# One block's weight conversions in a new order: a list for each step, more of them by hand at the start, and a place of their own for the narrowed chunks

## The chip, the cores and the metric

The kernel runs on one core of a Trainium2 chip. The metric is device time in microseconds; the median of three runs before the change is 604.85 us (604.66 to 604.88).

## The reference

Chunked attention, then a feed-forward layer with a rational activation, then a soft mixture of experts. With x the attention's output as 3072 tokens of 512:

```
h = x @ w_in                                   # 512 -> 2048
P = a0 + a1*h + a2*h^2 + a3*h^3
Q = 1 + |b0|*|h| + |b1|*h^2
g = P / (Q + 1e-6)
x2 = g @ w_out                                 # 2048 -> 512
logits = x2 @ phi                              # 512 -> 32 slots
d = softmax over tokens; c = softmax over slots
slot_out = experts(d.T @ x2);  out = c @ slot_out
```

w_in and w_out come in as float64. [...]

## The kernel before, in words

The 3072 tokens are 6 blocks of 512, and a block has 8 steps, one for each 256 of the 2048 columns of h. A step is numbered kk over all blocks; the first block is steps 0 to 7.

In a step, TensorE (PE) computes the **next** step's h (`h0`, `h1`: twelve 128x128x512 matmuls each, x and w_in each split into a high and a low part, L321). ScalarE (ACT) and VectorE (DVE) make the rational function of **this** step's h: `a1` is ACT L540, L541, L543 and DVE L542; `d1` is DVE L553, L554; `a2` is ACT L559, L560; `t` is DVE L570, L571 for the step before, after a product on GpSimd (POOL, L517). `p0`, `p1` transpose the finished g (L347, copied by ACT L348) and multiply it into the logits (L340). `at` runs one slice of the next block's attention; a block has two pairs of heads' tiles, 18 slices a pair: scores on PE (L164), softmax on DVE and ACT (L182, L185, L186, L190 to L192), transposes (L201, copied by ACT L205), values (L214), DVE L224, transposes (L233), and the copies into the next block's x, ACT L237 and DVE L238. At `h0` of a block's last step all slices that are left are run.

Only the first block also converts the weights, chunk by chunk (i = 0 to 7):

- `i`, `o`: load a chunk of w_in (L291) or w_out (L296) into one of four buffers of the pool `g`.
- `s` (split_w): f64_narrow (ACT L278, DVE L279, ACT L280, DVE L282) makes float32, then ACT L304 and DVE L305 the high and low part that h needs. h of step i reads chunk i.
- `n` (narrow_w_out): the same f64_narrow on a chunk of w_out, into one of three scratch tiles that are taken in turn; POOL L312 stores it to DRAM for the end of the kernel.
- `w` (wp_chunk), `z` (wp_sum): eight PE transposes of the narrowed chunk (L416), two ACT copies into a tile of pool S (L417), eight PE products with phi (L424), and one small ACT copy (L425). The logits need chunk i of it.

What sets the order: up to `start.close()` PE, ACT, DVE and POOL follow the program's order as written (table `pre`, which advances several generators in turn). After it the tile layer sorts each engine's instructions by a priority and by its own planning, so the rows printed below as the order are what counts. Each engine works through its own list strictly in order; an instruction that waits holds all behind it on that engine. Before, one list (`ord0`) with relative chunk numbers served all eight steps of the first block.

## Time and profile before

| | |
|---|---|
| median of 3 runs | 604.85 us |
| profiled execution, its own time | 606.56 us |
| its span, first to last instruction | 604.8 us |
| PE busy | 546.7 us, 90% |
| DVE busy | 454.2 us, 75% |
| ACT busy | 417.9 us, 69% |
| POOL busy | 125.3 us, 21% |
| a1 of step 0 / 1 / 5 / 8 starts at | 47.87 / 59.29 / 114.27 / 150.04 us |

The shares are averages over stages with different limits. The first block ends near 150 us; the five others take some 73 us each. PE's busy time counts a matmul from its start to a modelled end, so in the first block, where matmuls wait for little things between them, it reads fuller than it is.

### The profile page before, as it was taken

Reading aid. Unit: us, or ns where it says so; the run is one execution under the profiler, and the core shown is the slowest. Engines: PE = TensorE matmul, PEld = TensorE weight load, DVE = VectorE, ACT = ScalarE, POOL = GpSimd, SP = SyncE. Lnnn points to the kernel's source line nnn. Section 1 sums busy time; section 2 is a strip of 40 time slices with the busy share of each in tenths; the row PEclk is TensorE's granted clock in tenths of the full one; section 3 lists DMA queues with packets and bytes.
Section 4 is the critical chain, followed back from the end, with each engine's and each line's share of the span. In section 5 each row is a group of like instructions: output and inputs, shape, how many; then the busy total and the mean of one; then the engine's idle time right before and its main releaser. Section 6 shows DMA issues by size and latency. Waiting matters only on the chain.

```text
span 604.8 us, 13444 instructions
## 1 busy us (share of the span) xinstructions
PE 546.7 (90%) x5832; PEld 381.3 (63%) x5832; DVE 454.2 (75%) x559; ACT 417.9 (69%) x542; POOL 125.3 (21%) x65
## 2 busy tenths in 40 slices
PE   2679899979999999999999999999999997889981
PEld 2567676657767777677766777767777675435220
DVE  4667999987987988978889798897987969610031
ACT  2568999986877868778687777877778778410041
POOL 0000132122213133131331313223133315100000
PEclk9969899998999999999999999999999999788996
DMA  7975887230220222112122022220275235799938
GB/s 296 413 271 189 336 293 264 83 127 0 107 71 29 78 70 106 70 37 80 63 106 70 21 87 71 105 71 22 87 279 191 88 140 181 290 369 407 409 133 333
DMA packets 21755, 97.41 MB, mean 161 GB/s; under 512 B 3136, under 2 KB 3136, under 8 KB 16704
## 3 DMA queue, kind: packets, MB, share of 16 engines
q1 hardware_dynamic: 19728, 92.28, 41.2%
q0 software_dynamic: 1152, 4.19, 1.7%
q8 instruction: 46, 0.75, 0.5%
q10 hardware_dynamic: 816, 0.07, 0.1%
q14 instruction: 13, 0.11, 0.0%
HBM read 86.05 MB, written 10.49 MB: 160 GB/s over the span
## 4 chain that ended last, share of the span: by engine, by line
PE 54%; ACT 18%; DVE 13%; issue 5%; DMA 5%; POOL 2%; SPq 0%; DVEq 0%; ACTq 0%; POOLq 0%
PE h L321 28%; PE m L398 4%; ACT S L540 4%; ACT S L541 3%; ACT g L348 3%; PE lg L340 3%; PE m L347 3%; PE m L214 3%; DVE T L553 2%; PE h L640 2%; PE m L233 2%; POOL S L517 2%; PE m L201 2%; DMA xt<-in_kw_dram 2%; DMA T<-in_moe_w_dram 2%
## 5 line engine op out<-in xcount | busy, mean ns | idle before, releaser
L321 PE MATMUL h<-xt,win 128*128 128x512 f32 x1152 | 296.5, 405 | 7.7 <-ACT win L304 5.9
L321 PEld LDWEIGHTS h<-xt,win 128*128 128x128 f32 x1152 | 212.1, 191 | 56.2 <-ACT win L304 8.3
L517 POOL TENSOR_TENSOR S<-S,S 128x1024 f32<-128x1024 f32 (+1 forms) x49 | 118.9, 2428 | 317.1 <-DVE S L542 304.1
L540 ACT ACTIVATE S<-h,ctab 128x1024 f32<-128x1024 f32 (+1 forms) x49 | 53.9, 1100 | 58.7 <-PE h L321 56.6
L542 DVE SCALAR_TENSOR_TENSOR S<-S,S 128x1024 f32<-128x1024 f32 (+1 forms) x49 | 58.8, 1200 | 42.9 <-ACT S L541 42.7
L553 DVE TENSOR_TENSOR T<-T,h 128x1024 f32<-128x1024 f32 (+1 forms) x49 | 58.4, 1192 | 6.7 <-ACT T L543 6.7
L570 DVE SCALAR_TENSOR_TENSOR T<-T,ctab,S 128x1024 f32<-128x1024 f32 (+1 forms) x49 | 63.3, 1294 | 0.0
L347 PEld LDWEIGHTS m<-ident,T 128*128 128x128 f32 x384 | 44.0, 144 | 28.9 <-issue 13.4
L571 DVE SCALAR_TENSOR_TENSOR T<-S,T 128x1024 f32<-128x1024 f32 (+1 forms) x49 | 59.8, 1220 | 3.2 <-POOL S L517 0.5
L554 DVE SCALAR_TENSOR_TENSOR T<-T,ctab,h 128x1024 f32<-128x1024 f32 (+1 forms) x49 | 61.3, 1250 | 0.7
L543 ACT ACTIVATE T<-h,ctab 128x1024 f32<-128x1024 f32 (+1 forms) x49 | 59.2, 1208 | 0.0
L348 ACT ACTIVATE g<-m 128x512 f32<-128x512 f32 x96 | 53.8, 607 | 3.8 <-PE m L347 3.7
L560 ACT ACTIVATE S<-S,ctab 128x1024 f32<-128x1024 f32 (+1 forms) x49 | 55.9, 1140 | 0.8
L559 ACT ACTIVATE S<-S 128x1024 f32<-128x1024 f32 (+1 forms) x49 | 51.6, 1054 | 6.8 <-DVE S L542 5.1
L347 PE MATMUL m<-ident,T 128*128 128x128 f32 x384 | 54.3, 282 | 1.4 <-DVE a L185 1.2
L541 ACT ACTIVATE S<-h,ctab 128x1024 f32<-128x1024 f32 (+1 forms) x49 | 54.2, 1105 | 0.6 <-DVE T L570 0.6
L340 PE MATMUL lg<-T,wp 128*32 128x512 f32 x192 | 40.7, 618 | 3.9 <-DVE T L571 3.8
L398 PE MATMUL m<-g,ptok 128*32 128x512 f32 x192 | 23.5, 634 | 0.4 <-ACT ptok L390 0.4
L186 ACT ACTIVATE a<-a 128x512 f32<-128x512 f32 x22 | 13.8, 640 | 14.1 <-DVE a L185 14.1
L693 DVE TENSOR_SCALAR win<-h,csum 128x512 f32<-128x512 f32 x12 | 8.0, 744 | 20.4 <-PE m L687 20.4
L214 PE MATMUL m<-v,a 64*32 64x64 f32 x1408 | 20.8, 233 | 2.7 <-issue 2.5
L238 DVE TENSOR_TENSOR xt<-m,xt 128x512 fp32r<-128x512 f32 x24 | 16.3, 687 | 7.9 <-ACT xt L237 7.8
(152 smaller groups left out, 601.3 us busy)
## 6 DMA issues: line engine op xcount, KB each, us to landing
win<-in_moe_w_dram SPq DMA_DIRECT2D x32, 512.0 KB, 5.0
k<-in_kw_dram SPq DMA_DIRECT2D x11, 1024.0 KB, 7.4
v<-in_vw_dram SPq DMA_DIRECT2D x11, 1024.0 KB, 4.9
g<-in_moe_w_in_dram SPq DMA_DIRECT2D x8, 1024.0 KB, 6.5
g<-in_moe_w_out_dram SPq DMA_DIRECT2D x8, 1024.0 KB, 8.9
out_dram<-win SPq DMA_DIRECT2D x12, 512.0 KB, 6.1
q<-in_qw_dram SPq DMA_DIRECT2D x11, 512.0 KB, 3.7
T<-in_moe_w_dram SPq DMA_DIRECT2D x10, 512.0 KB, 10.3
```

The lines of the kernel that those rows point to most:

```text
L321: PE.matmul(tile_[:, f2, :], lhsT=ww[:, c, f2 * P:f2 * P + P], rhs=xx[:, c, :], start=(n == 0), stop=(n == 3 * NC - 1))
L340: PE.matmul(st["lg"][32 * j:32 * j + 32, :], lhsT=wp[:, 4 * qd + j, :], rhs=gt_tile[k - 1 + j // 2][:, j % 2, :], start=(qd == 0), stop=(q ...
L347: PE.transpose(pb[:, m, f2 * P:f2 * P + P], t_[:, f2, tt * P:tt * P + P], ident)
L348: ACT.activation(gts[b, qd][:, 2 * part:2 * part + 2, 2 * P * o:2 * P * o + 2 * P], pb, AF.Copy)
L517: POOL.tensor_tensor(out[:, o], q[:, o], w[:, o], ALU.mult)
L540: ACT.activation(s[:, o], hh[:, o], AF.Abs, scale=b0)
L541: ACT.activation(y[:, o], hh[:, o], AF.Square, scale=rb1)
L543: ACT.activation(t[:, o], hh[:, o], AF.Identity, bias=a2, scale=a3)
L553: DVE.tensor_tensor(t[:, o], t[:, o], hh[:, o], ALU.mult)
L554: behind[kk] = DVE.scalar_tensor_tensor(t[:, o], t[:, o], a1, hh[:, o], ALU.add, ALU.mult).ins
L570: DVE.scalar_tensor_tensor(t[:, o], t[:, o], a0, w[:, o], ALU.add, ALU.mult)
L571: DVE.scalar_tensor_tensor(t[:, o], e[:, o], 2.0, t[:, o], ALU.subtract, ALU.mult, reverse0=True)
```

## The change

- Each narrowed w_out chunk gets a tile of its own from the pool `win` (16 buffers) where three scratch tiles went round before. split_w takes its two `win` tiles only after narrowing.
- f64_narrow yields once more, between DVE L279 and ACT L280, so that a generator can be advanced in three pieces before its end.
- `pre` now holds, in hand order: the first two pairs' attention, splits of chunks 0 to 2, narrowing of w_out chunks 0 and 1, wp of chunk 0, and both halves of step 0's h. The loads of the next block's q and v move from `loads` into `pre`, behind those of w_in and w_out chunk 2.
- `ord0` is a list for each step, with absolute chunk numbers. The last conversion stands in step 4; before, the last ones stood in steps 6 and 7. Of 36 attention slices 15 stand in steps 0 to 4 and 21 in steps 5 to 7; before, six stood in each step.

```
-    'loads': "q0 q1 v0 i0 v1 o0 i1 o1 q2 v2".split(),
-    'pre': "A A B B A A A A A A A A A A B B B B s B B A A B B s A A A A s B B n t B B B B B B n t t".split(),
-    'pre2': "i2 w0 z0 o2 n1 i3".split(),
-    'ord0': "at a1 w1 s2 h0 d1 at t o3 z1 i4 n2 at a2 h1 p0 at p1 at at".split(),
+    'loads': "q0 q1 v0 i0 v1 o0 i1 o1".split(),
+    'pre': ("A A B B A A A A A A A A A A B B B B s B B s A A B B s A A A A n n B B B B s i2 t B B B B t n n o2 t q2 v2 "
+            "N N h0 t i3 w0 N N o3 h1 u u u u i4 z0").split(),
+    'ord0': [x.split() for x in (
+        "at a1 n2 o4 h0 d1 t s3 i5 a2 w1 h1 z1 p0 p1",
+        "at a1 n3 o5 h0 d1 t s4 i6 w2 a2 n4 o6 h1 z2 p0 at p1",
+        "at a1 n5 o7 w3 h0 d1 t at s5 i7 z3 w4 a2 h1 z4 p0 at p1",
+        "at a1 n6 w5 h0 d1 t at s6 z5 a2 h1 p0 at p1 at",
+        "at a1 n7 w6 h0 d1 at t s7 z6 at w7 a2 h1 z7 p0 at p1 at",
+        "at at a1 h0 d1 at t at a2 h1 p0 at p1 at at",
+        "at at a1 h0 d1 at t at a2 h1 p0 at p1 at at at",
+        "at a1 h0 d1 at t at a2 h1 p0 at p1 at at")],
...
         DVE.tensor_scalar(f, f, -F64_HI, F64_HI, ALU.max, ALU.min)
+        yield
         ACT.activation(f, f, AF.Prelu, scale=2.0 ** -112, alpha=-(2.0 ** 32))
...
-    scratch = [p_win("win", [P, 1024]) for _ in range(3)]
...
-        wh, wl = win[i] = [p_win("win", [P, NC, 2 * P], F32R) for _ in range(2)]
         src = stage_in.pop(i)
         yield from f64_narrow(src[:, :, :, 1], src)
+        wh, wl = win[i] = [p_win("win", [P, NC, 2 * P], F32R) for _ in range(2)]
...
-        f = scratch[i % 3].rearrange("p (j d) -> p j d", j=2)
+        f = p_win("win", [P, 1024]).rearrange("p (j d) -> p j d", j=2)
...
-            "s": split_w(0), "n": narrow_w_out(0), "t": split_w(1)}
-    for what in KN["pre"]:
-        next(gens[what], None)
...
+            "s": split_w(0), "t": split_w(1), "u": split_w(2), "n": narrow_w_out(0), "N": narrow_w_out(1)}
...
+    for what in KN["pre"]:
+        if what in gens:
+            next(gens[what], None)
+        elif what[0] == "h":
+            if what == "h0":
+                hs[0] = ps_h("h", [P, 2, BLK])
+            h_part(0, hs[0], int(what[1]))
+        elif what[0] in "qv":
+            load(what)
+        else:
+            convert(what)
...
-            convert(what[0] + str(min(i + int(what[1]), NSTEP)))
+            convert(what)
```

The lines of the changed kernel stand 8 to 10 further down: L278 becomes L286, L280 L289, L304 L312, L305 L313, L417 L425, L424 L432, L425 L433, L540 L550, L542 L552.

**PE, h of step 0.** h_592 before and h_559 after are the same tile; win_415 and win_416 (win_521 and win_522) are chunk 0's two parts, L416 (L424) are wp's transposes and L424 (L432) its products. Before:

```order
L321 MATMUL h_592<-xt_150,win_416 128x512 x2
L416 MATMUL m_561<-ident_103,win_145 128x128 x4
L416 MATMUL m_567<-ident_103,win_145 128x128 x4
L321 MATMUL h_592<-xt_150,win_416 128x512
L424 MATMUL m_573<-u_107,S_560 128x32 x4
L321 MATMUL h_592<-xt_150,win_416 128x512
L321 MATMUL h_592<-xt_150,win_415 128x512 x4
L321 MATMUL h_592<-xt_151,win_415 128x512
L424 MATMUL m_573<-u_107,S_560 128x32 x4
L321 MATMUL h_592<-xt_151,win_415 128x512 x3
L321 MATMUL h_592<-xt_150,win_416 128x512 x4
```

After:

```order
L329 MATMUL h_559<-xt_147,win_522 128x512 x4
L424 MATMUL m_579<-ident_103,win_448 128x128 x4
L424 MATMUL m_585<-ident_103,win_448 128x128 x4
L329 MATMUL h_559<-xt_147,win_521 128x512 x4
L329 MATMUL h_559<-xt_148,win_521 128x512 x4
L329 MATMUL h_559<-xt_147,win_522 128x512 x4
L432 MATMUL m_617<-u_107,S_578 128x32 x4
```

The products with phi, which stood inside the second half of h, now stand behind it.

**ACT, from a1 of step 2 on.** S and T are the rational function's tiles, g_... loaded chunks, a_4 attention. Before (h_809 is step 2's h):

```order
L540 ACTIVATE S_948<-h_809,ctab_105 128x1024
L541 ACTIVATE S_950<-h_809,ctab_105 128x1024
L280 ACTIVATE g_728<-g_728 128x1024
L543 ACTIVATE T_949<-h_809,ctab_105 128x1024
L278 ACTIVATE g_740<-g_740 128x1024
L280 ACTIVATE g_740<-g_740 128x1024
L417 ACTIVATE S_955<-m_956 128x512
L417 ACTIVATE S_955<-m_962 128x512
L278 ACTIVATE g_831<-g_831 128x1024
L425 ACTIVATE wp_106<-m_997 128x64
```

After (h_789):

```order
L286 ACTIVATE g_702<-g_702 128x1024
L289 ACTIVATE g_702<-g_702 128x1024
L433 ACTIVATE wp_106<-m_932 128x64
L425 ACTIVATE S_942<-m_943 128x512
L425 ACTIVATE S_942<-m_949 128x512
L569 ACTIVATE S_955<-S_873 128x1024
L433 ACTIVATE wp_106<-m_970 128x64
L570 ACTIVATE S_955<-S_955,ctab_105 128x1024
L312 ACTIVATE win_926<-g_702 128x1024
L194 ACTIVATE a_4_867<-a_4_867 128x8x64
L550 ACTIVATE S_986<-h_901,ctab_105 128x1024
```

Two wp chunks and chunk 5's split now stand between the a1 of steps 2 and 3, and the second wp copy has one full instruction between it and the copies whose product it reads.

**DVE, up to the last copies into the next block's x (xt).** T_1590 after belongs to step 7, a_9 to the last attention pair. Before:

```order
L282 SCALAR_TENSOR_TENSOR win_146<-g_1288 128x1024
L238 TENSOR_TENSOR xt_618<-m_1478,xt_617 128x16x32
L238 TENSOR_TENSOR xt_618<-m_1516,xt_617 128x16x32
L542 SCALAR_TENSOR_TENSOR S_1523<-S_1525,S_1523 128x1024
L553 TENSOR_TENSOR T_1524<-T_1524,h_1444 128x1024
L305 TENSOR_TENSOR win_1437<-g_1167,win_1436 128x1024
```

After:

```order
L552 SCALAR_TENSOR_TENSOR S_1589<-S_1591,S_1589 128x1024
L199 TENSOR_SCALAR sm_1474<-sm_1474 128x8
L232 TENSOR_TENSOR a_9_1587<-m_1519,sm_1468 128x8x64
L200 RECIPROCAL sm_1474<-sm_1474 128x8
L563 TENSOR_TENSOR T_1590<-T_1590,h_1452 128x1024
L232 TENSOR_TENSOR a_9_1587<-m_1520,sm_1474 128x8x64
L564 SCALAR_TENSOR_TENSOR T_1590<-T_1590,ctab_105,h_1452 128x1024
L580 SCALAR_TENSOR_TENSOR T_1446<-T_1446,ctab_105,S_1478 128x1024
L246 TENSOR_TENSOR xt_629<-m_1597,xt_628 128x16x32
L246 TENSOR_TENSOR xt_629<-m_1604,xt_628 128x16x32
```

Before, the copies into xt stood ahead of step 6's own work and of the last conversion; now the conversion is long done and the copies stand behind most of step 7.

## Rows read from the trace of the kernel before

**Rows 1.** Windows: us, busy us (count) of PE, PEld, DVE, ACT, POOL; clock; DMA.

```profile
59.30:114.30 55.00, 50.29 (x510) 37.64 (x509) 51.64 (x62) 52.05 (x67) 12.79 (x8) 0.97 0.70 249
151.40:500.00 348.60, 344.68 (x3761) 252.01 (x3761) 298.32 (x345) 271.19 (x346) 89.76 (x38) 1.00 0.25 89
```

**Rows 2.** Chain that ended last, 30 to 155 us: start, us, what.

```profile
30.28 1.23 DVE win L305
31.50 1.21 DVE g L279 x2
...
33.96 1.98 PE m L233 x8
...
36.62 4.63 PE h L321 x10
...
43.07 0.81 PE m L424 x8
...
46.15 1.69 PE h L321 x7
...
119.76 2.89 DVE g L279
...
136.35 2.50 DVE win L305
138.89 10.58 PE h L321 x40
...
151.48 0.92 PE m L164 x61
```

**Rows 3.** Timeline of ACT, step 0: start, us, instruction, idle before.

```profile
47.87 1.11 ACT L540 ACTIVATE S<-h,ctab 128x1024 f32<-128x1024 f32 x1 [1.45 <-PE h L321]
...
49.88 1.21 ACT L543 ACTIVATE T<-h,ctab 128x1024 f32<-128x1024 f32 x1
50.97 0.60 ACT L417 ACTIVATE S<-m 128x512 f32<-128x512 f32 x1
51.44 1.19 ACT L278 ACTIVATE g<-g 128x1024 uint32<-128x1024 uint32 x1
...
55.10 1.06 ACT L559 ACTIVATE S<-S 128x1024 f32<-128x1024 f32 x1
56.05 1.12 ACT L304 ACTIVATE win<-g 128x1024 fp32r<-128x1024 f32 x1
57.05 0.23 ACT L425 ACTIVATE wp<-m 128x64 f32<-128x64 f32 x1
...
58.24 1.14 ACT L560 ACTIVATE S<-S,ctab 128x1024 f32<-128x1024 f32 x1
59.29 1.09 ACT L540 ACTIVATE S<-h,ctab 128x1024 f32<-128x1024 f32 x1
```

**Rows 4.** Timeline of ACT, a1 of step 5.

```profile
114.27 1.14 ACT L540 ACTIVATE S<-h,ctab 128x1024 f32<-128x1024 f32 x1
```

**Rows 5.** Timeline of DVE: half-width and full-width instructions one behind another.

```profile
87.36 1.28 DVE L238 TENSOR_TENSOR xt<-m,xt 128x512 fp32r<-128x512 f32 x2
...
146.22 1.23 DVE L542 SCALAR_TENSOR_TENSOR S<-S,S 128x1024 f32<-128x1024 f32 x1 [3.67 <-ACT S L541]
147.36 1.22 DVE L553 TENSOR_TENSOR T<-T,h 128x1024 f32<-128x1024 f32 x1
148.62 1.28 DVE L554 SCALAR_TENSOR_TENSOR T<-T,ctab,h 128x1024 f32<-128x1024 f32 x1
149.81 1.28 DVE L570 SCALAR_TENSOR_TENSOR T<-T,ctab,S 128x1024 f32<-128x1024 f32 x1
```

**Rows 6.** Timeline of PE: h at full clock, transposes behind a pause, matmuls behind a pause.

```profile
33.96 1.97 PE L233 MATMUL m<-ident,T 128*128 128x128 f32 x8 [3.41 <-DVE T L224]
...
69.75 3.27 PE L321 MATMUL h<-xt,win 128*128 128x512 f32 x7 [2.33 <-ACT win L304]
...
152.33 3.01 PE L321 MATMUL h<-xt,win 128*128 128x512 f32 x12
```

**Rows 7.** Windows again: the granted clock (eighth number group) in two low stretches.

```profile
35.00:40.00 5.00, 4.31 (x13) 3.23 (x12) 3.65 (x4) 3.55 (x5) 0.73 (x1) 0.50 0.39 131
70.00:75.00 5.00, 5.00 (x137) 3.73 (x137) 5.00 (x8) 5.00 (x7) 0.00 (x0) 0.67 0.64 234
```

**Rows 8.** Waits, ACT, 59.3 to 114.3 us: who waited for whom, us, times, longest.

```profile
ACT wp L425 <- PE m L424: 2.7, 3, 1.0
```

More of the change, by code (lines that the diff above doesn't have):

```diff
@@ L455, in tile_chunk_attention__rational__soft_moe @@
     gens = {"A": attention(0, after=NPAIR), "B": attention(1, lambda shape: p_T("T", shape), after=NPAIR),
-            "s": split_w(0), "n": narrow_w_out(0), "t": split_w(1)}
-    for what in KN["pre"]:
-        next(gens[what], None)
-    for gen in gens.values():
-        for _ in gen:
-            pass
-    start.close()
-    for what in KN["pre2"]:
-        load(what) if what[0] in "qv" else convert(what)
+            "s": split_w(0), "t": split_w(1), "u": split_w(2), "n": narrow_w_out(0), "N": narrow_w_out(1)}
     total = NBLK * NSTEP
     hs, gt_tile = {}, {}
-    hs[0] = ps_h("h", [P, 2, BLK])
-    h_part(0, hs[0], 0)
-    h_part(0, hs[0], 1)
+    for what in KN["pre"]:
[9 more added lines that the diff above has]
+            convert(what)
+    for gen in gens.values():
+        assert next(gen, None) is None
+    start.close()
     state = {"att": None}
@@ L593, in tile_chunk_attention__rational__soft_moe @@
             state["att"] = attention_block(b + 1)
-        for what in KN["ord0" if b == 0 else "ord" if b < NBLK - 1 else "ordz" if kk == total - 1 else "ordl"]:
+        for what in KN["ord0"][i] if b == 0 else KN["ord" if b < NBLK - 1 else "ordz" if kk == total - 1 else "ordl"]:
             run_step(kk, what)
```

## Prediction

> **What bounds the kernel now.** I read the windows first. From 151.4 us on PE is busy 344.68 of 348.60 us at full clock [rows 1]: five of the six blocks run at PE's pace, the change touches none of their instructions, and whatever the first block gains or loses is passed on whole. So the question is when PE gets to the point where both kernels do the same again: h of step 8 is done, and the scores of the next attention pair (L164) begin. Before, that is 151.48 [rows 2].
>
> The chain of waits, read in order of time, says what set it. Up to 36.62 the first two pairs' attention ends, with DVE's row of small work on the way to the transposes at 33.96; then h of step 0 with wp's products inside it [rows 2]. From there it lies almost wholly on ACT: in the window 59.3 to 114.3 ACT is busy 52.05 of 55.00 us [rows 1], and the largest of its waits is for wp's products, 2.7 us in three [rows 8]. Near the end it leaves ACT twice for DVE: L279 of 2.89 us, and L305 of 2.50, behind which PE starts h of step 7 at 138.89 and runs on through h of step 8 [rows 2]. So: startup, then ACT, then the last conversion.
>
> ACT's work in the first block is the same before and after, instruction for instruction. The change can win only by starting it earlier, by filling ACT's waits, or by shortening what follows the last conversion. I go through the stages with prices taken from neighbours' starts, since ACT overlaps them by about 0.1 us [rows 3]: a1 and a2 of a step together 5.1 us (L540 and L541 2.01, L543 1.09, L559 0.95, L560 1.05); a narrowing activation 1.19 long, so 1.07; L304 1.0; L417 0.47; L425 0.1 (0.23 long); the half-width attention and g copies 0.5, priced as L417.
>
> **Startup.** On DVE one L305 and one L279 no longer stand ahead of the last attention copies: 1.23 + 0.6 = 1.8 us earlier [rows 2], so h of step 0 starts at 34.8 for 36.62. The high part of chunk 0 is written later than before (ACT now narrows w_out chunk 0 first), but by my count of ACT's list at 32.6, before the x it is multiplied with. The first twelve matmuls fall in the low clock: ten took 4.63 [rows 2], so 5.6; eight transposes (1.97 at the low clock [rows 6], half at the full one; I take 1.2) and the other twelve, at the full-clock rate of 3.01 [rows 6], end h at 44.6. Wp's products, of which the chain has two pieces of 0.81 [rows 2], are no longer inside. So a1 of step 0 stands at 44.6 for 47.87 [rows 3]: 3.3 us won.
>
> **Step 0 to 1.** ACT's list holds a1 and a2 (5.1), five narrowing activations (5.35), one L304, one L425 and two L417: 12.5, and I count 0.6 of wait for a product on PE: a1 of step 1 at 57.7 for 59.29. Two narrowing activations more have been put in there, so this is still ahead.
>
> **Steps 1 to 4, the dense stretch.** Between a1 of step 1 and a1 of step 5 ACT's list now holds four steps' a1 and a2 (20.4), 18 narrowing activations (19.3), five L304 (5.0), twelve L417 (5.6), seven L425 (0.7) and eleven half-width copies (5.5): 56.5 us; all conversions are in it. ACT's waits come on top. Before they were 55.00 - 52.05 = 2.95 [rows 1]. Following the list I find more: the L425 of wp chunks 1, 4 and 6 have one full instruction between them and the copies that feed their product, less than the products take (0.6 + 1.35 + 0.6 by the list), and two copies of g wait for transposes that stand behind pieces of h (1.1 + 1.4): 5.4 with small ones. I take the middle, 4.2, since ACT's first pieces may overlap better than my list shows. So a1 of step 5 stands at 57.7 + 56.5 + 4.2 = 118.4, for 114.27 [rows 4]. It is later because more was done before it.
>
> **Steps 5 to 8.** Here the change moves the bound. No conversion is left, but 21 of 36 attention slices are, and the last copies into x (L238, two) stand on DVE behind most of step 7; h of step 8 needs them. DVE's list from step 5's L542 (2.1 us behind a1) to the last of them has 14 full-width instructions at 1.2 (three intervals of 3.59 from 146.22 to 149.81) and eleven half-width ones at 0.64 [rows 5], and 0.5 of tiny ones, an estimate: 24.3 us, nearly gapless, since ACT and PE hand it the operands about when it is free. That ends at 118.4 + 2.1 + 24.3 = 144.8. Of h of step 8 twenty matmuls follow, 5.0 at full clock [rows 6], and four transposes, 0.5: 150.3, which is 1.2 before 151.48 [rows 2].
>
> **Clock.** PE then has a pause of about 3.4 us (values of the last pair done, waiting for two L224 on DVE), transposes, and h. The nearest row is 33.96: a pause of 3.41 us, eight transposes [rows 6], and then ten matmuls in 4.63 with the clock at 0.50, that is 1.2 GHz; later in the same h seven took 1.69 [rows 2, 7]. The same ten slow ones here lose 10 x (0.46 - 0.25) = 2.1 us. The other bound is 138.89, 40 matmuls in 10.58 where the full rate gives 10.0 [rows 2, 6]: 0.6. I take 2.1, because the pause ahead is like the first row's. The Trainium skill (TensorE: Matmul & The Clock Gate, section "HAM oscillation — how this bites in real kernels") counts half of the time at the lower clock as lost. By it the 4.63 would cost an estimated 2.3, and the sum would be 0.2 higher; the matmul rows agree with it.
>
> **What costs nothing.** No load ends a wait of ACT before, and chunks are now asked for at their buffer's last reader, far ahead of use; the cover is the two or three us that each list has before the chunk's narrowing, and a late one would cost its lateness. Its own tile for each w_out chunk takes a wait for a store off DVE and puts a similar one at the last split, where DVE has 3 us of slack. The long L279 and L305 (2.89 and 2.50 [rows 2], where a neighbour of L305 takes 1.23 [rows 2]) ran while POOL multiplied; the new list has one such neighbour pair, in step 1, under ACT's work. Their going is in the sum, which uses undisturbed prices.
>
> **Sum.** -1.2 + 2.1 = +0.9 us. On the profiled span of 604.8 that is 605.7; the execution itself took 606.56, 1.76 more than its span and 1.71 more than the median, so I put the shift on the median of 604.85: **605.8 us**. Its own range, with ACT's waits between 2.95 and 5.4, the clock term between 0.6 and 2.1, and 1 us of error in the list either side, is 602.0 to 608.0. That is a forecast of nothing that can be told: about 0.2% (1.2 us) is what a measurement of this kernel separates from no change. The 3.3 us won at the start and what the last conversion no longer holds up go into the longer stretch with DVE at the end.
>
> **Rivals.**
> *PE runs free: faster.* In the dense stretch h is ready long before ACT needs it, so products may be done whenever ACT comes to copy them; then ACT's waits lie between 0 and 2.95, and if PE keeps its clock the last part costs no extra. The end is 57.7 + 56.5 + 1.5 + 31.9 (2.1 + 24.3 + 5.0 + 0.5) = 147.6, 3.9 earlier: 601.0, between 599.5 and 602.5. For it: ACT waited little in a similar list before [rows 8], and the two long DVE instructions on the old chain go. Against: the distances of one instruction in the new list.
>
> *The clock falls in the dense stretch: slower.* PE now waits for ACT's L417 in steps 2, 3 and 4 with all of h done. At 69.75 a pause of 2.33 us was followed by seven matmuls in 3.27 [rows 6], where the full rate gives 1.75, at a mean clock of 0.67 [rows 7]: 1.5 a pause. I count four pauses of 2.0 to 3.2 us. If each delays the product that ACT waits for, the sum grows by 6.0 to 611.8. It decides from the point where the pause outlasts the instructions that ACT has between copy and L425. Against it: two of the four have two or more instructions of cover.
>
> *It doesn't do what it says.* The scheduler could have put the conversions back; the printed order shows that it didn't, so no chance goes there.
>
> **Chances.** Forecast 0.48 (0.05 of it faster by over 0.2%, 0.21 the same, 0.22 slower), free PE 0.36, falling clock 0.16. That gives faster 0.41, the same 0.21, slower 0.38. Both signs are open; the likeliest case's own range stands above. The range for 8 in 10 goes from 599.5, the free PE's lower end, to 609.5, which leaves out the upper half of the falling clock.
>
> **What would show it.** Right: a1 of step 0 at 44 to 45.5, of step 1 near 57.7, of step 5 at 117 to 120, last L305 before 123; a PE pause of 3 to 4 us ahead of the last attention transposes, a clock under 0.8 in the window around h of step 8, and L164 behind it at 152 to 154. Free PE: a1 of step 5 before 116.5 and no low clock. Falling clock: windows under 0.8 between 65 and 115 and L425 waits above 6 us. The forecast is wrong at its root if ACT isn't the bound between steps 1 and 5, or if something past 155 us moves.

## The result, and the profile after

The changed kernel takes 610.43 us (median of 5 runs, 607.63 to 611.06). The kernel before took 604.88 beside it (5 runs, 604.66 to 606.15). The ratio is 1.008, with an interval of 1.0059 to 1.0101: slower by 0.8%, where 605.8 us was forecast and the range ended at 609.5. The two profiled executions are 4.1 us apart (610.64 with a span of 608.9, against 606.56 with 604.8), the medians 5.6.

In the changed kernel the lines are shifted: a1's first instruction L540 is L550, wp's copy L417 is L425, its products L424 are L432 and their copy L425 is L433, h is L329, the copies into x L246, the g copies L356, the scores L172. Here are a1 of steps 0, 1, 5 and 8 on ACT (start, us, instruction, idle before and its releaser), to be read against [rows 3, 4]:

```profile
43.15 1.12 ACT L550 ACTIVATE S<-h,ctab 128x1024 f32<-128x1024 f32 x1 [0.18 <-PE h L329]
56.09 1.11 ACT L550 ACTIVATE S<-h,ctab 128x1024 f32<-128x1024 f32 x1
...
121.79 1.12 ACT L550 ACTIVATE S<-h,ctab 128x1024 f32<-128x1024 f32 x1
...
155.59 1.11 ACT L550 ACTIVATE S<-h,ctab 128x1024 f32<-128x1024 f32 x1 [6.60 <-PE h L329]
```

The start is 4.7 us earlier than before (43.15 for 47.87) and 3.2 us at step 1. By step 5 it is 7.5 us late (121.79 for 114.27). Of these 7.5 the forecast had 4.1 (118.4 for 114.27), because more conversions stand ahead of step 5 now; the other 3.4 are the miss. Steps 5 to 8, which hold no conversion any more, win back 3.1. The windows after (columns as in [rows 1]; the third from the end is the granted clock):

```profile
56.09:121.79 65.70, 59.13 (x441) 47.97 (x441) 52.70 (x54) 57.60 (x75) 13.36 (x9) 0.90 0.54 196
155.86:500.00 344.14, 339.22 (x3734) 247.37 (x3734) 293.71 (x341) 266.96 (x340) 89.07 (x37) 1.00 0.25 87
```

```profile
65.00:70.00 5.00, 3.50 (x17) 3.51 (x18) 5.00 (x5) 5.00 (x7) 0.59 (x1) 0.61 0.83 282
70.00:75.00 5.00, 5.00 (x21) 4.20 (x21) 5.00 (x7) 5.00 (x7) 0.53 (x1) 0.70 0.98 400
...
95.00:100.00 5.00, 5.00 (x20) 4.47 (x20) 4.88 (x6) 4.21 (x7) 0.31 (x1) 0.50 0.26 105
...
145.00:150.00 5.00, 4.47 (x16) 3.93 (x17) 5.00 (x6) 2.07 (x4) 0.52 (x1) 0.50 0.00 2
150.00:155.00 5.00, 5.00 (x20) 4.02 (x19) 0.18 (x1) 0.00 (x0) 0.00 (x0) 0.85 0.00 0
```

ACT is busy 57.60 of the 65.70 us between those two a1 and idle 8.10, where before it was idle 2.95 of 55.00 [rows 1]. Behind 155.86 the kernel is the old one again: PE busy 339.22 of 344.14 at full clock. Now the clock stands at 0.50, the 1.2 GHz level, from 95 to 100 and again from 145 to 150, and it is low from 65 to 75. What ACT waited for between 57 and 122 us (us in total, times, longest):

```profile
ACT wp L433 <- PE m L432: 3.9, 4, 1.3
ACT g L356 <- PE m L355: 3.4, 3, 1.4
ACT S L425 <- PE m L424: 0.6, 1, 0.6
```

Before, L425's waits for the same products were 2.7 [rows 8]. The chain of waits, which lay almost wholly on ACT before, now runs through PE from 66.50 to 84.16 and from 92.68 to 103.75. Some of its rows:

```profile
66.50 3.62 PE m L432 x16
...
92.68 1.23 PE m L432 x8
94.39 1.55 PE m L432 x8
95.94 1.33 PE m L355 x6
97.27 0.85 PE h L329 x2
```

The pauses ahead of two of these rows, by the timeline of PE:

```profile
66.50 3.62 PE L432 MATMUL m<-u,S 128*128 128x32 f32 x16 [4.07 <-ACT S L425]
...
92.68 1.23 PE L432 MATMUL m<-u,S 128*128 128x32 f32 x8 [1.98 <-ACT S L425]
```

Sixteen wp products take 3.62 us at 66.50, behind a pause of 4.07, and from 92.68 on, behind a pause of 1.98, wp's products, transposes and pieces of h come one by one while ACT waits. These two are the only pauses of PE over half a microsecond between a1 of step 1 and a1 of step 5. The end of the block, on PE (start, us, instruction):

```profile
145.53 1.97 PE L241 MATMUL m<-ident,a 128*128 128x128 f32 x8 [3.76 <-DVE a L232]
147.29 1.06 PE L355 MATMUL m<-ident,T 128*128 128x128 f32 x4
148.19 7.30 PE L329 MATMUL h<-xt,win 128*128 128x512 f32 x24
155.33 0.60 PE L355 MATMUL m<-ident,T 128*128 128x128 f32 x4
155.86 0.86 PE L172 MATMUL m<-k,q 64*32 64x64 f32 x64
```

The last two copies into x run on DVE from 147.77 to 149.05, h of step 8 waits for them, and L172 follows at 155.86, 4.4 us behind the 151.48 of before [rows 2].

### The profile page after: what moved, and what is told of

Same layout as the page of the kernel before. It is cut to its first block, busy times and chain, and to the rows that moved or that the text cites. A ratio compares the mean times of both kernels' runs of the same rounds, so it can differ in the third digit from the quotient of the medians.

```text
span 608.9 us, 13436 instructions
## 1 busy us (share of the span) xinstructions
PE 546.1 (90%) x5832; PEld 384.7 (63%) x5832; DVE 450.5 (74%) x559; ACT 418.8 (69%) x542; POOL 123.9 (20%) x65
## 4 chain that ended last, share of the span: by engine, by line
PE 55%; ACT 16%; DVE 13%; DMA 5%; issue 5%; POOL 2%; SPq 0%; DVEq 0%; ACTq 0%; POOLq 0%
PE h L329 28%; PE m L355 4%; PE m L406 4%; ACT S L550 4%; ACT S L551 3%; ACT g L356 3%; PE lg L348 3%; PE m L432 3%; PE m L222 3%; DVE T L563 2%; PE h L650 2%; PE m L209 2%; POOL S L527 2%; DVE T L564 2%; PE m L241 2%
## 5 line engine op out<-in xcount | busy, mean ns | idle before, releaser
L329 PE MATMUL h<-xt,win 128*128 128x512 f32 x1152 | 295.2, 405 | 2.9 <-ACT xt L245 1.7
L329 PEld LDWEIGHTS h<-xt,win 128*128 128x128 f32 x1152 | 213.3, 192 | 50.2 <-DVE T L564 2.3
L527 POOL TENSOR_TENSOR S<-S,S 128x1024 f32<-128x1024 f32 (+1 forms) x49 | 117.5, 2398 | 338.9 <-DVE S L552 324.0
L552 DVE SCALAR_TENSOR_TENSOR S<-S,S 128x1024 f32<-128x1024 f32 (+1 forms) x49 | 58.8, 1200 | 53.1 <-ACT S L551 52.9
L550 ACT ACTIVATE S<-h,ctab 128x1024 f32<-128x1024 f32 (+1 forms) x49 | 53.9, 1101 | 61.4 <-PE h L329 58.3
L355 PEld LDWEIGHTS m<-ident,T 128*128 128x128 f32 x384 | 45.5, 147 | 28.4 <-issue 14.4
L356 ACT ACTIVATE g<-m 128x512 f32<-128x512 f32 x96 | 54.0, 603 | 8.0 <-PE m L355 7.7
L355 PE MATMUL m<-ident,T 128*128 128x128 f32 x384 | 55.8, 286 | 3.4 <-DVE a L193 2.3
L348 PE MATMUL lg<-T,wp 128*32 128x512 f32 x192 | 38.4, 608 | 4.6 <-DVE T L581 4.5
L432 PEld LDWEIGHTS m<-u,S 128*128 128x128 f32 x128 | 18.3, 219 | 10.1 <-ACT S L425 9.7
L432 PE MATMUL m<-u,S 128*128 128x32 f32 x128 | 18.7, 297 | 6.6 <-ACT S L425 6.5
(152 smaller groups left out, 598.7 us busy)
```

The lines of the kernel that those rows point to most:

```text
L329: PE.matmul(tile_[:, f2, :], lhsT=ww[:, c, f2 * P:f2 * P + P], rhs=xx[:, c, :], start=(n == 0), stop=(n == 3 * NC - 1))
L355: PE.transpose(pb[:, m, f2 * P:f2 * P + P], t_[:, f2, tt * P:tt * P + P], ident)
L356: ACT.activation(gts[b, qd][:, 2 * part:2 * part + 2, 2 * P * o:2 * P * o + 2 * P], pb, AF.Copy)
L527: POOL.tensor_tensor(out[:, o], q[:, o], w[:, o], ALU.mult)
L550: ACT.activation(s[:, o], hh[:, o], AF.Abs, scale=b0)
L552: DVE.scalar_tensor_tensor(s[:, o], y[:, o], QC, s[:, o], ALU.add, ALU.add)
```

## The experiments

Two causes stood against each other first. Theory A: the late attention loses, since 21 of 36 slices lie in steps 5 to 8 and PE has to wait for the last of them. Theory B: the dense conversions lose, since ACT waits among them. A stand-in, below, is a matmul added to the program whose result is overwritten unread: work beyond the reference. All ratios are to the kernel before, on the same chip and beside it. Its median was 604.88 beside the changed kernel (5 runs each) and 605.6 to 606.0 beside the others (16 to 25 runs); the first line is the last of these batches. "Clock missing" is the sum over the twenty-one 5-us windows from 55 to 160 of 5 us x (1 - granted clock). It is that of one execution, the profiled one, which need not be the median: e1's took 612.63.

| kernel | us, median (range) | ratio to before | clock missing |
|---|---|---|---|
| before | 605.82 (604.3 to 607.1) | 1 | 3.4 |
| changed | 610.43 (607.6 to 611.1) | 1.0080 [1.0059, 1.0101] | 10.2 |
| e6_late | 612.75 (611.7 to 614.1) | 1.0114 [1.0082, 1.0146] | 8.6 |
| e1_spread | 605.16 (604.3 to 612.6) | 1.0000 [0.9971, 1.0029] | 18.8 |
| e2_paced | 604.44 (601.9 to 606.2) | 0.9970 [0.9950, 0.9990] | 8.5 |
| e12_two | 612.14 (610.9 to 617.3) | 1.0122 [1.0088, 1.0155] | 8.5 |
| e4_hold | 605.95 (605.4 to 607.8) | 1.0003 [0.9988, 1.0018] | 6.8 |
| e5_order | 609.27 (608.4 to 610.5) | 1.0063 [1.0046, 1.0079] | 10.2 |
| e17_order4 | 608.90 (607.2 to 610.9) | 1.0057 [1.0037, 1.0078] | 10.2 |
| e7_dense_hold | 606.82 (605.6 to 607.9) | 1.0019 [1.0008, 1.0031] | 5.1 |
| e9_zlater | 606.80 (604.6 to 609.5) | 1.0020 [1.0004, 1.0036] | 8.7 |
| e15_sum | 602.38 (601.5 to 603.9) | 0.9948 [0.9931, 0.9964] | 1.7 |
| e10_spread_hold | 600.37 (599.1 to 602.3) | 0.9917 [0.9899, 0.9936] | 1.7 |
| e8_paced_hold | 600.03 (598.7 to 600.8) | 0.9902 [0.9884, 0.9919] | 3.4 |
| e16_half | 605.89 (604.5 to 607.3) | 1.0000 [0.9989, 1.0012] | 6.8 |
| e11_inpause | 607.57 (605.3 to 609.8) | 1.0030 [1.0013, 1.0047] | 13.7 |
| e14_paced2 | 600.88 (599.3 to 603.4) | 0.9921 [0.9898, 0.9944] | 3.4 |
| e13_before_hold | 607.10 (604.5 to 609.2) | 1.0023 [1.0004, 1.0043] | 5.2 |

### Late attention, or dense conversions

**e6_late** is the kernel before with the change's distribution of attention slices alone (1, 2, 3, 4, 5, 7, 8, 6 in steps 0 to 7, for six in each):

```diff
-    'ord0': "at a1 w1 s2 h0 d1 at t o3 z1 i4 n2 at a2 h1 p0 at p1 at at".split(),
+    'ord0': one list for each step, the same but for the number of "at"
```

> The kernel before, with the attention slices of the first block counted as in the change (1, 2, 3, 4, 5, 7, 8, 6 by step) and nothing else changed. Theory A: slower by 3 to 6 us, 608 to 611, with a pause of PE ahead of h of step 8. Theory B: within 1.5 us of before, 603.5 to 606.5, since the conversions of the last steps hold PE up anyway.

**e1_spread** is the changed kernel with six slices in each step and everything else of the change:

```diff
-        "at a1 n2 o4 h0 d1 t s3 i5 a2 w1 h1 z1 p0 p1",
+        "at a1 n2 o4 h0 d1 at t s3 i5 at a2 w1 h1 z1 p0 at p1 at at",
...
-        "at at a1 h0 d1 at t at a2 h1 p0 at p1 at at at",
+        "at a1 h0 d1 at t at a2 h1 p0 at p1 at at",
```

> The changed kernel, with six attention slices in each step of the first block as before (18 or so fall into steps 0 to 2), the conversions where the change put them. Theory A, late attention: the change loses because 21 of 36 slices stand in steps 5 to 7, so that DVE's list ends 25 us behind a1 of step 5's L542 and PE stands still ahead of h of step 8. Then the pause ahead of step 8's h goes, h of step 8 follows h of step 7 at once, and the time falls by 4 to 6 us, to 604 to 607. Theory B, dense conversions: the loss is ACT's waits in steps 1 to 4. Then a1 of step 5 only comes later, by the 3 us of attention that ACT has to do earlier, what is won at the end is spent ahead of it, and the time stays at 608 to 611.

**e2_paced** spreads the conversions too: own places and the new start of the change, but one w_out chunk and at most one split a step, six slices in each:

```diff
+        "at a1 n2 o4 h0 d1 at t s3 i5 at a2 w1 h1 z1 p0 at p1 at at",
+        "at a1 n3 o5 h0 d1 at t s4 i6 at a2 w2 h1 z2 p0 at p1 at at",
+        "at a1 n4 o6 h0 d1 at t s5 i7 at a2 w3 h1 z3 p0 at p1 at at",
+        "at a1 n5 o7 h0 d1 at t s6 at a2 w4 h1 z4 p0 at p1 at at",
+        "at a1 n6 w5 h0 d1 at t at a2 z5 w6 h1 z6 p0 at p1 at at",
+        "at a1 n7 w7 h0 d1 at t s7 at a2 h1 z7 p0 at p1 at at",
```

> The changed kernel with its start and its own places, but from step 0 on one chunk of w_out and one split a step (w_out chunks 2 to 7 in steps 0 to 5, splits 3 to 6 in steps 0 to 3 and split 7 in step 5, one wp chunk a step, two in step 4), and six attention slices a step. Theory A: as with the attention spread alone, 604 to 607. Theory B: ACT's waits in steps 1 to 4 fall from some 8 us to about 3, and the early start is kept: 599 to 603, faster than the kernel before.

Late attention alone costs 1.1%, some 7 us, more than A expected, and taking it out of the change gives back 0.8%. That is A's result twice, and e6 has the pause ahead of step 8 that A named, although there the clock stays at 1.00 behind it. On PE in e6:

```profile
150.56 1.09 PE L241 MATMUL m<-ident,a 128*128 128x128 f32 x8 [3.01 <-DVE a L232]
```

B's number for e1 (608 to 611) is excluded, and e2 fell short of B's 599 to 603. But e1's profiled execution was the longest of its ten, 612.63 with the clock at 0.50 to 0.58 from 65 to 75, 85 to 100 and 120 to 130. Over the whole execution its mean granted clock was 0.939; the nine others had 0.955 to 0.972 and took 604.3 to 606.7. So there was a third suspect, TensorE's clock.

### The pause ahead of step 8

**e4_hold** is the changed kernel with 14 stand-ins, put between the last products of the attention values and the transposes:

```diff
+                    if nxt == NSTEP:
+                        for n in range(14):
+                            PE.matmul(hs[nxt][:, n % 2, :], lhsT=win[7][0][:, n % NC, 0:P], rhs=xt[0][0][:, n % NC, :],
+                                      start=True, stop=True)
+                        while state["att"] is not None:
+                            slice_()
```

> The changed kernel with 14 stand-in matmuls 128x128x512 in front of the last attention slices of the first block, written to the bank that h of step 8 overwrites; they fall into PE's pause ahead of step 8's h. If the low clock behind that pause costs what the rows say, h of step 8 falls from 7.30 us to about 5.8, the window around it shows a clock near 1.00, and the time falls by 1 to 2 us. If the clock there costs nothing (theory: h waits for x anyway), the time stays within 0.5 us.

It gave back 4.7 us by the ratios (0.0077 of 605.8), more than I expected of the clock. But the scheduler also changed its order: 20 score products of block 1 (L172) now stand inside h of step 8. Two more kernels were to separate the two, the same edit with 1 and with 4 stand-ins.

> e4_hold took back about 4.5 of the 5.6 us by which the changed kernel is behind. Two things were in it: the work of TensorE ahead of step 8 that held the clock, and a new order on TensorE, in which the first score products of block 1 (L172) and one of step 9's products stand inside step 8's products instead of behind them. This kernel keeps the order as far as it goes and has one stand-in product instead of the fourteen. If the clock was the gain: 609 to 610.5, with the granted clock at 0.5 to 0.85 around step 8's products and their 24 taking 7 us or more. If the order was: 605.5 to 606.5 all the same. If each had its part: 607 to 608.5.

> e4_hold with 4 stand-in products instead of 14: the order on TensorE around step 8 is that of e4_hold (20 score products of block 1 inside step 8's products), and some 2.7 us of the pause ahead of step 8 stay. If e4_hold gained by the order: 605.5 to 606.5. If by the clock: 608.5 to 610, with a granted clock of 0.5 to 0.85 around step 8's products. In between: both.

With one stand-in the order fell back to the changed kernel's, so e5 says nothing on the order; it is a second copy of the changed kernel (1.0063), and against it e4's gain is 3.6 us. With four the order behind the stand-ins is that of e4_hold, ACT's and DVE's too, and most of the gain is gone (1.0057): the clock's number, not the order's. Windows 145 to 150 and h of step 8 in e17 and then in e4:

```profile
145.00:150.00 5.00, 5.00 (x21) 4.27 (x19) 4.29 (x5) 1.80 (x3) 0.00 (x0) 0.50 0.00 0
```

```profile
144.63 1.97 PE L241 MATMUL m<-ident,a 128*128 128x128 f32 x8 [3.10 <-DVE a L232]
...
147.29 2.07 PE L329 MATMUL h<-xt,win 128*128 128x512 f32 x4
```

```profile
145.00:150.00 5.00, 4.09 (x42) 3.14 (x42) 5.00 (x6) 2.52 (x5) 0.59 (x1) 1.00 0.02 7
```

```profile
145.60 1.09 PE L241 MATMUL m<-ident,a 128*128 128x128 f32 x8 [0.82 <-DVE a L232]
...
147.43 1.19 PE L329 MATMUL h<-xt,win 128*128 128x512 f32 x4 [0.30 <-ACT xt L245]
```

The pause of 3.10 us with 4 stand-ins leaves the clock at 0.50; filled to 0.82, it stays at 1.00, and eight transposes take 1.09 for 1.97. From a1 of step 5 to a1 of step 10 is 49.90 us in the changed kernel, 49.61 in e17 and 47.51 in e4. So 2.1 us of these 2.4 are the clock, which is the value that the prediction's clock term had, and 0.3 the order. The rest of the gain by the ratios lies outside this stage, and the traces do not say where. The Trainium skill (TensorE: Matmul & The Clock Gate, section "HAM oscillation — how this bites in real kernels") counts half of the time at the lower clock as lost; the windows of e17 from 140 to 155 stand at 0.85, 0.50 and 0.97, which by that rule would be an estimated 3.4 us. The trace gives 2.1; part of the time at the low clock is the pause itself (PE is busy 1.90 of the 5.00 us from 140 to 145), where nothing is lost.

### ACT's waits in the dense stretch

**e7_dense_hold** puts stand-ins ahead of the products of wp chunks 2 and 5; **e9_zlater** moves the products of chunks 2 to 7 one or two places further behind the copies that feed them:

```diff
# e7_dense_hold
+        for n in range({2: 14, 5: 8}.get(i, 0)):
+            PE.matmul(pb_, lhsT=win[0][0][:, n % NC, 0:P], rhs=xt[0][0][:, n % NC, :], start=True, stop=True)
# e9_zlater
-        "at a1 n3 o5 h0 d1 t s4 i6 w2 a2 n4 o6 h1 z2 p0 at p1",
-        "at a1 n5 o7 w3 h0 d1 t at s5 i7 z3 w4 a2 h1 z4 p0 at p1",
-        "at a1 n6 w5 h0 d1 t at s6 z5 a2 h1 p0 at p1 at",
-        "at a1 n7 w6 h0 d1 at t s7 z6 at w7 a2 h1 z7 p0 at p1 at",
+        "at a1 n3 o5 h0 d1 t s4 i6 w2 a2 n4 o6 h1 p0 at p1",
+        "at a1 z2 n5 o7 w3 h0 d1 t at s5 i7 w4 a2 z3 h1 p0 at p1",
+        "at a1 z4 n6 w5 h0 d1 t at s6 a2 h1 p0 z5 at p1 at",
+        "at a1 n7 w6 h0 d1 at t s7 w7 z6 at a2 h1 p0 z7 at p1 at",
```

> The changed kernel with 14 stand-in products ahead of the second chunk's wp products and 8 ahead of the fifth's (into the bank that those products then fill), where TensorE paused 4.1 and 2.0 us and the granted clock was 0.61 to 0.70 and 0.50 behind it. Theory C, the ACT waits of the dense stretch that the prediction missed come from the low clock behind the pauses: the wait for the g copies around 101 to 104 and for the product at 96 go, a1 of step 5 starts at 119 to 120 instead of 121.8, and the time is 607.5 to 609. Theory D, they come from where copy, product and copy stand on the two queues: a1 of step 5 at 121.5 or later and 610 to 611.

> The changed kernel with the products of wp chunks 2 to 7 one or two list places later, so that ScalarE has other work between its copy of a chunk (L425) and the copy of the product (L433). Theory D (the waits come from the places): the four waits of L433 in steps 1 to 5, 3.9 us in all, fall below 1.5, a1 of step 5 starts at 119 to 120 and the end of the block comes as much earlier: 607 to 609. Theory C (low clock): the waits move to other copies, 609.5 to 611.

Each gives back 0.6%: 3.7 and 3.6 us, or 2.7 and 2.6 against e5, the copy of the changed kernel that ran beside them. a1 of step 5 starts at 119.53 and 117.46, but that is no clean sign: a1 of step 1, ahead of both edits, already stands at 55.02 and 54.55 instead of 56.09, and e5 and e17 have a1 of step 5 at 120.37 and 120.92 with neither edit. Cleaner is the stretch from a1 of step 1 to a1 of step 5. It is 65.0 to 65.7 us in the four traces that have the change's code there (changed, e4, e5, e17), 64.51 in e7 and 62.91 in e9. Its windows in e7 and e9, and ACT's two largest waits in e7's:

```profile
55.02:119.53 64.51, 60.14 (x465) 47.56 (x463) 52.54 (x54) 57.38 (x75) 13.40 (x9) 0.97 0.58 207
```

```profile
54.55:117.46 62.91, 56.54 (x438) 45.67 (x438) 52.53 (x54) 56.65 (x73) 13.38 (x9) 0.92 0.60 213
```

```profile
ACT wp L436 <- PE m L435: 5.0, 4, 2.0
ACT g L356 <- PE m L355: 1.3, 2, 0.9
```

In e7 the granted clock over the stretch is 0.97 for 0.90, while ACT's order is the changed kernel's but for one wp copy, and DVE's is the same. The g copies then wait 1.3 us instead of 3.4, as C had it. But wp's copies wait 5.0 instead of 3.9 (0.7 of it at chunk 2, whose product the stand-ins themselves put later), and ACT is still idle for 7.13 us (64.51 - 57.38) of the 8.10. So holding the clock alone, by stand-ins, takes 0.5 to 1.2 us off the stretch; of the 4.2 us between the two profiled executions (spans 608.9 and 604.7) the other 3.0 lie outside it. e9 has the low clock still (0.92) and takes 2.1 to 2.8 off: the places, D, have the larger part, although the waits of L433 fell only to 2.8, not below 1.5 as D had it. **e15_sum** joins e9's places, 14 stand-ins at chunk 2, and e4's edit.

> e9_zlater's places for the wp products, 14 stand-ins behind the pause at 61 to 65, and e4_hold's 14 stand-ins ahead of step 8, all on the changed kernel. Alone they gave back 3.6, 3.6 and 4.5 us. If they are separate losses on one chain, the sum ends at 600 to 602; if the first two are the same waits (those behind the low clock), at 603 to 604.5; if all three are one loss, at 605.5 to 607.

Its stretch is 60.66 us, and the whole kernel 602.38: 8.0 us less than the changed one (0.0132 of 605.8), of 3.7 + 3.6 + 4.7 = 12.0 if all were separate. It lies just above the expectation for three separate losses: by the ratios they overlap by a third. The stages do not show that overlap. The stretch is 5.0 us shorter, where e7 and e9 alone take 1.2 and 2.8, and a1 of step 5 to a1 of step 10 is 47.94 us, 2.0 shorter, where e4 alone takes 2.4. Window of the stretch and ACT's waits in it:

```profile
56.98:117.64 60.66, 54.88 (x451) 45.30 (x452) 52.47 (x54) 56.65 (x74) 13.41 (x9) 0.97 0.60 213
```

```profile
ACT wp L436 <- PE m L435: 2.8, 2, 1.7
ACT a L213 <- PE m L209: 0.7, 1, 0.7
ACT g L356 <- PE m L355: 0.2, 1, 0.2
ACT S L425 <- PE m L424: 0.2, 1, 0.2
```

ACT is busy 56.65 and idle 4.01, where e9, with the same order on ACT and DVE, was idle 6.26: once the places are moved, holding the clock takes 2.2 us off the stretch. The g copies, 3.4 us of wait in the changed kernel, wait 0.2, as in e9. Two of their three waits there (1.01 and 1.43 us, up to 101.26 and 103.78) stood behind PE's work at 0.50 from 95 to 100; the third (0.94, up to 120.81) stood at full clock.

### Both together, and the best kernels

**e10_spread_hold** is e7_dense_hold's code with e1's six slices a step, so between e7 and e10 only the place of the attention differs.

> e1_spread (the change's conversions, six attention slices in each step) with 14 stand-ins behind the pause of the second wp chunk and 8 near the fifth. If late attention and low clock are separate losses: 600 to 602 (e1's 605.2 less what the stand-ins gave e2_paced, 4.4). If the low clock was all that the spread list lost, and the rest is bound by ScalarE and VectorE: 603 to 605.

600.37 against 606.82: 1.0019 falls to 0.9917, which is 6.2 us for late attention, the low clock behind its pause included (0.64 and 0.67 from 140 to 150 in e7). PE shows it: no pause ahead of step 8, and h of steps 7 and 8 at the full rate with only PE's own transposes and logits' products between them.

```profile
131.58 5.72 PE L329 MATMUL h<-xt,win 128*128 128x512 f32 x24
...
139.08 5.74 PE L329 MATMUL h<-xt,win 128*128 128x512 f32 x24
```

**e8_paced_hold** is e2_paced with 18 stand-ins ahead of the products of wp chunk 2 (the edit of e7 with `{2: 18}`); **e16_half** has 9. **e11_inpause** writes 18 stand-ins into the logits' bank, right behind the transposes of that chunk.

> e2_paced with 18 stand-in products in the 5.2 us in which TensorE waited there for the copy of wp chunk 2 (62.2 to 67.4), behind which the granted clock was 0.50 to 0.65 from 65 to 80 and VectorE waited 3.5 us for an attention product. If the clock's fall costs time there: that wait falls to 1.5 or less, and 601.5 to 603. If it is hidden: 604 to 605 as before; and above 605.5 if the stand-ins themselves delay the product.

> e8_paced_hold with 9 stand-ins instead of 18. If its gain is the clock's coming back at 75 instead of 80, then with half the dense work behind the pause the clock may come back later and 601 to 604 follows, in step with the low windows between 65 and 85; if the gain is only that some products stand later in TensorE's order, 600 to 601 whatever the clock.

> e2_paced with the 18 stand-in products in a bank that is free at that time (that of the logits), so that they needn't wait for the copy of wp chunk 2. In e8_paced_hold they started only when the pause was over (67.7), ran 6.6 us at the low clock and put the wp product 6.5 us later, and yet the kernel was 5 us faster. If the clock is what was gained: no window below 0.9 between 60 and 80, the wp product at 67 to 69, and 598 to 600. If it was the later place of that product and of what follows it: 604 to 605 as e2_paced.

e8 is the fastest of all, below its expectation, 1.0% below the kernel before (interval 0.8 to 1.2%) and 1.8% below the changed one, although its stand-ins did not fill the pause: they waited for the same bank as the product behind them and ran when the pause was over. On PE:

```profile
67.71 6.62 PE L432 MATMUL m<-xt,win 128*128 128x512 f32 x18 [5.18 <-ACT S L425]
74.17 1.87 PE L435 MATMUL m<-u,S 128*128 128x32 f32 x16
```

The window 75 to 80, in e2 and then in e8:

```profile
75.00:80.00 5.00, 5.00 (x104) 4.15 (x103) 3.09 (x4) 5.00 (x6) 1.08 (x1) 0.50 0.39 125
```

```profile
75.00:80.00 5.00, 4.78 (x149) 3.90 (x149) 3.42 (x4) 3.93 (x6) 3.22 (x1) 1.00 0.52 180
```

e2 stays at 0.50 to 80 with PE busy all the time, in small products and transposes; e8 is back at 1.00 by 75, and no later window to 160 is below it. In e11 the scheduler spread the stand-ins ahead of the pause, a pause of 3.27 us remained, a second of 3.44 followed at 84.2 to 87.6, and the clock is low from 65 to 80 and from 85 to 100: 607.57. My expectation for it had a condition that the kernel did not meet, so it doesn't tell what filling that pause would give. In e16 the clock is back at 0.97 between 70 and 75, and e16 is yet no faster than the kernel before and 0.3% slower than e2, at the edge of the noise. Its rows show a second fall:

```profile
82.73 0.66 PE L241 MATMUL m<-ident,a 128*128 128x128 f32 x4 [1.97 <-DVE a L232]
```

```profile
85.00:90.00 5.00, 5.00 (x23) 4.82 (x22) 4.06 (x5) 2.92 (x6) 0.00 (x0) 0.50 0.51 206
90.00:95.00 5.00, 5.00 (x74) 3.35 (x72) 4.17 (x4) 5.00 (x6) 2.07 (x1) 0.58 0.63 210
```

With 9 fewer products PE comes to the attention's transposes at 80.76, waits 1.97 us for DVE there (e8 starts the same transposes at 82.66 without a wait), and the clock falls again; from a1 of step 3 to a1 of step 5, where these windows lie, e16 takes 36.15 us, e8 29.92 and e2 31.47. So neither of my two readings is shown. Against "the clock at 75 instead of 80" speaks that at a1 of step 3 e2 and e8 still stand level (87.45 and 87.68): e8 gets ahead only later, by 2.9 us at step 4 and 3.8 at step 6, where e2's lowest window is 0.73. And the stand-ins changed more than the clock: the scheduler put ACT's work in another order too (in e2 the copy of chunk 2's product, at 72.34, stands ahead of a1 of step 2, at 73.74; in e8 it comes at 76.07, behind a1 at 71.68). Whether e8 gained by the clock or by the order is not separated.

**e14_paced2** moves products and the last narrowing of e8 away from ACT's remaining waits; **e13_before_hold** puts 10 and 6 stand-ins ahead of wp products 1 and 7 in the kernel before.

> e8_paced_hold with the wp products from chunk 3 on a place later and the last w_out chunk narrowed at the end of step 4 instead of in step 5. In e8_paced_hold ScalarE still waited 1.9 us in step 4 for products and transposes and 2.5 us in step 5 for the transposes of the last chunk, which waited for VectorE's narrowing. If these waits lie on the path: 597 to 599. If VectorE's list behind them is the bound: 599.5 to 600.5.

> The kernel before with stand-in products ahead of wp products 1 (10 of them) and 7 (6), near the two places where its granted clock fell (0.67 in 70 to 75; 0.81 to 0.84 in 135 to 145). If holding the clock is worth as much there as in the paced kernel, 600 to 602. By its own windows the loss is 1 to 1.5 us at most: 604 to 605.5; more than 606 if the stand-ins are in the way.

e14 is no faster than e8 (0.9921 and 0.9902, intervals overlapping): what waits there is not on the path, or came back elsewhere. e13 is slower than the kernel before by 0.2%: its stand-ins took the fall at 70 to 75 away and brought one at 80 to 85 (0.50) and one at 120 to 125 (0.70). So stand-ins as such are no gain. What e8's needs beside them (the new start, the chunks' own places, the pacing) these runs do not separate.

**e12_two** takes the third piece of the narrowing away and leaves all else of the change:

```diff
         DVE.tensor_scalar(f, f, -F64_HI, F64_HI, ALU.max, ALU.min)
-        yield
         ACT.activation(f, f, AF.Prelu, scale=2.0 ** -112, alpha=-(2.0 ** 32))
```

> The changed kernel with the narrowing in two pieces as before the change; the rest of the change stays. Should the third piece matter (a conversion's ScalarE and VectorE steps interleave with other work in the startup), a1 of step 0 starts 0.5 to 1.5 us later than 43.1 and the time is 611 to 612. Should it not: 609.5 to 611.

a1 of step 0 starts at 47.52 instead of 43.15, three times what I allowed, and the kernel is 0.4% slower than the changed one by the two ratios, whose intervals overlap a little. PE, ahead of h of step 0 (h is L328 here):

```profile
35.52 1.97 PE L241 MATMUL m<-ident,T 128*128 128x128 f32 x8 [2.79 <-DVE T L232]
38.26 5.12 PE L328 MATMUL h<-xt,win 128*128 128x512 f32 x12 [0.77 <-ACT xt L245]
```

h starts at 38.26 where the changed kernel's chain has it at 34.86, behind transposes that waited for DVE. So with this list nearly all of the early start hangs on the third piece: with two, each entry of the startup's list issues more of a conversion, and more of it stands ahead of the last attention work (a list written for two pieces was not tried). In its profiled execution, the fastest of six, little of that is left by step 5: a1 starts there at 122.27, 0.5 us behind the changed kernel's 121.79.

## Why the prediction was wrong, step by step

- **Startup.** h of step 0 at 34.8 came at 34.86. Its first twelve products took 4.62 instead of 5.6, and the transposes and the other twelve 0.6 less than forecast, so a1 of step 0 stood at 43.15 for 44.6 and a1 of step 1 at 56.09 for 57.7: right in kind, 1.6 us too cautious.
- **Steps 1 to 4: the step that failed.** 56.5 of work and 4.2 of waits, 60.7, were forecast; 57.60 and 8.10, 65.70, were measured. The work was 1.1 off, the waits by 3.9: the term that was mis-sized is ACT's waits. My list had counted 5.4, and I took 1.2 off for an overlap that did not come. The list was right in kind and too short. For wp's products it had three waits, 2.55; four came, 3.9. For the g copies it had two, 2.5; three came, 3.4. A wait of 0.6 for a chunk's transposes it did not have. It was counted at PE's full speed, and PE was at 0.50 to 0.70 in three of the windows; but holding the clock alone (e7) leaves 7.1 of the 8.1 us, so the clock is the smaller part of the miss. Moving the products (e9) leaves 6.3, and both together (e15) 4.0. That e15's 60.66 is my sum to the tenth is chance: it is another program. How much of each single wait was the clock and how much the place is not separated.
- **The rival that came nearest.** "The clock falls in the dense stretch" gave 611.8 for the 610.43 measured, but its number is near by luck. Its windows below 0.8 between 65 and 115 are there (0.61, 0.70, 0.50). Its four pauses of 2.0 to 3.2 us are two, 4.07 and 1.98. Its other sign, over 6 us of waits for wp's products alone, is not there: 3.9, and 3.4 more at the g copies, which it did not name. And it put 6.0 us on the low clock in the stretch, where holding the clock takes 1.2 (e7), or 2.2 once the products are moved (e15 beside e9).
- **Steps 5 to 8.** From a1 of step 5 to the last copy into x 26.4 us were forecast and 27.26 measured (149.05 - 121.79). Then 7.6 to L172 with the clock term, and 6.81 measured (155.86 - 149.05). That the bound moves to DVE and the last attention slices was right, and so was the low clock behind the pause of 3.76. What I did not see is that this tail is what the change pays with: against an even spread it loses 5 to 7 us (e1 beside the changed kernel; e10 beside e7; e6).
- **The sum.** +0.9 was forecast at L172 and +4.4 measured, of which the dense stretch, with the start's 1.6 taken off, is 3.4. The spans differ by 4.1. The medians differ by 5.6, because the profiled execution before lay 1.7 above its median and the one after only 0.2: by putting the shift on a median of three runs I lost another 1.4. In the later batches the kernel before had medians of 605.6 to 606.0, so part of this is the small number of runs.

Of the signs named ahead, the pause of 3 to 4 us, the clock under 0.8 behind it and the last L305 before 123 (118.27) came; a1 of step 5 at 117 to 120 (121.79) and the scores behind step 8 at 152 to 154 (155.86) did not, both for the time lost in the dense stretch.

What stays open: where the gains of e4 and e7 lie that their own stages don't show, and so how 12.0 us by the ratios become 8.0; what the chunks' own places are worth, which no run changes alone; and what the pause at 62 to 67 costs if it is really filled, since in e8 it is not and e11 failed to.

## What to carry to other kernels

Packing one engine's work tighter here lengthened the pauses of the engine that waits for it (on PE to 4.07 and 3.76 us, where the kernel before had 2.33 at the most between a1 of step 1 and a1 of step 8). Count the waits by the distances on both engines' lists, and do not shorten the count for an overlap that no row shows: that alone was 1.2 us. Then price what stands behind a pause at the lower clock; behind the last pause that was 2.1 us. Where a copy waits for a product, moving it a few places down the list was worth more than keeping the clock up (each alone, 2.1 to 2.8 us against 0.5 to 1.2 in the stretch).

Move optional work (here the attention of the next block) early or evenly, not behind the last stage that needs it: with the same stand-ins, the same conversions lost 0.2% with it late (e7) and won 0.8% with it even (e10). Stand-in products are worth a try behind a known pause, but look at where the next pause goes, and at what they do to the scheduler's order: 18 gave 0.7% on the paced kernel, 9 cost 0.3% at the edge of the noise, and 16 on the kernel before cost 0.2%.

## What the runs showed of the hardware that I had not expected

A pause need not be long to be followed by a low clock: 1.98 us on PE ahead of 92.68 in the changed kernel and 1.97 us in e16 were each followed by a window at 0.50. Nor does a pause's length alone decide it: behind the 3.01 us of e6_late the windows from 150 to 160 stand at 1.00. And a busy PE does not always bring the clock back at once: in e2 PE shows no idle time from 67.4 to 80 and the clock stays at 0.50 for the two windows from 70 to 80, while behind 18 products of 512 columns in e8 it is at 1.00 from 75. Some DVE instructions that run beside POOL's L530 (in e8 from 60.21 for 3.29 us and from 91.70 for 2.41) are longer, with one input or two: a L287 with one took 2.28 where others take 0.69, a L291 with two 2.60 where the next took 1.21. DVE in e8:

```profile
61.78 2.28 DVE L287 TENSOR_SCALAR g<-g 128x1024 f32<-128x1024 f32 x1
...
92.59 2.60 DVE L291 SCALAR_TENSOR_TENSOR win<-g 128x1024 uint32<-128x1024 uint32 x1
...
97.50 1.21 DVE L291 SCALAR_TENSOR_TENSOR g<-g 128x1024 uint32<-128x1024 uint32 x1
```
